# Chunk-selecting attention and a squared-relu FFN in one kernel: who clears a tile, and in which order the FFN's steps are queued

## The chip, the core and the metric

The kernel runs on one core of one Trainium2 chip. The metric is the device time of one execution in microseconds. Before the change it is 281.74 us, the median of three runs (281.1 to 281.81).

## The reference, cut to what matters

```
B, H, S, D = 4, 8, 768, 64          # q, k, v: float32
ub   = sum_d max(q * k_min(chunk), q * k_max(chunk))     # bound of each query on each 32-row chunk
top  = the 6 chunks with the highest ub, of those not after the query's own chunk
attn = softmax(q k^T / 8, over the rows of the chosen chunks that are not after the query)
x    = (attn v), laid out as [3072 tokens, 512]
h    = relu(x @ w_in)               # w_in 512 x 2048
out  = (h * h) @ w_out              # w_out 2048 x 512, out float32
```

## The kernel before, in words

**Tiling.** A sequence is cut into two halves of 384 rows. The eight halves (four batches) are done in the order of `ORDER`; halves 0, 1, 4 and 6 are first halves of a sequence (`half == 0`: 768 score columns a head), halves 2, 3, 5 and 7 second halves (1920 columns a head). A half has four head pairs; one pair of one half is a *slot*, so there are 32 slots, 0 to 31, and half n holds slots 4n to 4n+3. All matmuls are bf16.

**The steps of a slot.** The order of instructions on each engine is the order of the program (the schedule is manual); semaphores are put in where one engine reads what another wrote, and where a buffer is used again.

- `step_T` (in `step_P`, called two slots ahead) transposes k and q of a pair on TensorE (`tk`, `tq`, lines 244 and 251). `relus_T` makes `qr` from `tq` on ScalarE (line 272), `extrema` the chunks' extrema on VectorE (lines 217 to 219), and `place` copies the transposed k and q into `kq` (line 277; k mostly on VectorE, q on ScalarE). From half 3 on the transposes are DMAs and `relus` runs on VectorE (lines 300, 301).
- `step_U` (one slot ahead) makes the bounds `ub` on TensorE (lines 351, 355); VectorE takes the top 8 (MAX8, line 362) and writes which chunks are out (line 363) into `qn0` for half 0, into one of the three `nsel` tiles after that.
- `step_V` transposes that on TensorE (`qt`, line 379 or 390) and VectorE copies it into `kq` beside q (lines 384, 394, 395): a chunk that is out gets a large negative score by the matmul itself.
- `step_E` does one bank of scores on TensorE (`ps`, line 408) and its exponential on ScalarE (`e`, line 413); after the last bank of a head POOL cuts the diagonal blocks (line 417).
- `step_F`, one slot later, multiplies by v (`po`, line 433); VectorE divides (lines 442, 443) and writes `x`.

The places that chunk codes don't reach must be zero: `qn0` is cleared by POOL (line 150), the three `nsel` tiles by ScalarE (`blank`, line 191).

**The FFN.** When a half's `x` is complete it is transposed to `xT` (on TensorE for halves 0, 1 and 7, `x_T`, by DMA for the others), and `push` queues the half's FFN steps: 16 *steps up* (`ffn_up`: four matmuls `ph`, 128 x 384, relu on ScalarE to `ht`, square on VectorE to `h`) and 12 *steps down* (`ffn_down`: four matmuls `py`, 128 x 512, each reading one `h`; four steps to an output tile of 128 tokens, then a copy `ob` on ScalarE or VectorE and a store). The slots of the next half take steps from the queue by `f1()` at fixed places between their own steps, at most `quota` a slot. In the tail, after slot 31, the queue is emptied.

**Order of the queue before.** `push` puts eight steps down of the half before ahead of and between the sixteen up of its own half, and then the first four down of its own (`LAG = 4`); the other eight wait in `downs` for the next push. `quota` is 4 a slot in slots 4 to 7 (half 1), and 8, 6, 7, 7 in the four slots of each later half.

**Buffers.** PSUM: `ps` three buffers (`psS`), `ph` two (`psF`), `py` one (`psY`), the rest two (`psA`). The transposes of slots 6 to 8 use `psY` for k and `psS` for q.

**Loads.** POOL's queue issues nearly all loads, in the order of `later`, which `go` empties slot by slot: `w_in` in slot 0, k and q of half 2 in slot 2, the two halves of `w_out` in slots 3 and 4, the codes of half 2 in slot 4.

**The first slots** are written out by hand ahead of the loop: casts, clears, transposes, and runs of matmuls on `ident` (`busy`) that fill TensorE's waits.

Of the kernel before, what the change touches and what calls it, by code (L numbers as in the profile page):

```python
# [12 lines left out]
ACT = mybir.ActivationFunctionType  # L13
# [18 lines left out]

TP = 4
PP = HB // TP

LAG = 4


@with_exitstack
def kernel(  # L40
# [104 lines left out]
        nc.vector.memset(vn[i][:, :, :, D:D + 1], 1.0)  # L145
    ident = consts.tile([128, 128], BF16, tag="ident")
    make_identity(nc, ident)

    for c in (0, 3):
        nc.gpsimd.memset(qn0[:, :, :, c, :], 0.0)  # L150
    load_packed("k", 0, 4)
    for j in range(HT):
        for h in range(2):
# [31 lines left out]
    codes(0, 0, nc.vector.tensor_copy, 0, 1)  # L185

    warm = consts.tile([128, 1], F32, tag="warm")
    nc.scalar.activation(warm, hmask[:, 0, 0, 0:1], ACT.Exp)

    def blank(i):  # L190
        nc.scalar.mul(nsel[i].rearrange("p j h d -> p (j h) d"),
                      ident[:, 0:D].unsqueeze(1).to_broadcast([128, 2 * HT, D]), 0.0)

    def clear():

# [141 lines left out]
    def step_P(s):  # L337
        if s // NP >= ON_PE:
            relus(s)
            return  # L340
        step_T(s, *((S_, Y) if s == NP + 1 else (F, Y) if s < NP + 2 else
                    (Y, S_) if s < 2 * NP + 1 else (S_, A)))
        if s >= NP + 2 and s != 2 * NP + 1:
            step_T2(s)

# [100 lines left out]
            st.pop(s)  # L446

    queue = []
    downs = []
    h2 = {}  # L450

    xTs = {}
# [34 lines left out]
    def push(hb):  # L487
        xT = xTs.pop(hb)
        xs.pop(hb)
        ups = [lambda act, f=f: ffn_up(hb, xT, f) for f in range(NFI)]  # L490
        for c in ("u" * NFI) if hb == 0 else "dddd" + "uuud" * 4 + "uuuu":
            queue.append((ups if c == "u" else downs).pop(0))
        downs.extend(ffn_downs(hb, int(hb == 2 * B - 1)))
        if hb < 2 * B - 1:
            queue.extend(downs.pop(0) for _ in range(LAG))

    def ffn_downs(hb, tail=False):
        py = {}
        return [lambda act, t=t, c=c: ffn_down(hb, py, t, c, act, tail)
                for t in range(HT - tail) for c in range(4)]  # L500
# [75 lines left out]
        at(0, load_w_in, 1024 * g, 1024 * g + 1024)  # L576
    for j in range(HT):
        at(1, load_vt, 1, j)
    for n in "kq":
        at(2, load_packed, n, 2)  # L580
    at(4, codes, 0, 1, nc.gpsimd.dma_start)
    for g in range(2):
        at(3 + g, load_w_out, 8 * g, 8 * g + 8)
    for j in range(HT):
        at(6, load_vt, 0, HT + j)
        at(7, load_n, "k", 3, j)
# [31 lines left out]

    busy(28)
    step_cast("k", 0)  # L620
    blank(1)
    step_cast("q", 0)
    blank(2)
    clear()
    go(-1, 99)
    step_P(0)
    busy(10)
    step_T2(0)
    place(0, "k", nc.scalar.copy)
    blank(0)  # L630
    step_U(0)
    busy(9)
    step_cast("k", 1)
# [3 lines left out]
    step_cast("q", 1)  # L637
    step_P(1)
    step_T2(1)
    early.close()  # L640
    late = ctx.enter_context(tc.tile_pool(name="late", bufs=2))
    for s in range(NP):
        last = s + 1 == NP
        if s:
            step_E(s, 0, 0)
            step_E(s, 0, 1)
        step_E(s, 1, 0)
        busy(8)
        step_U(s + 1)
        if last:  # L650
            place(s + 1, "k", nc.vector.tensor_copy, 0, 1)
        else:
            place(s + 1, "k", nc.scalar.copy)
        step_E(s, 1, 1)
        if last:
            place(s + 1, "q", nc.scalar.copy)
            place(s + 1, "k", nc.scalar.copy, 1, 2)
        if s:
            step_F(s - 1, 0)
            step_F(s - 1, 1)  # L660
        if last:
            x_T(0, 0, F)
        step_V(s + 1)
        step_P(s + 2)
        if last:
            x_copy(0, 0, 0, 2, nc.vector.tensor_copy)
            busy(10, *F)
        else:
            relus_T(s + 2)
            extrema(st[s + 2]["k"], s + 2)  # L670
        go(s, 99)
    parts = []
# [5 lines left out]
    for s, (b, half, p) in enumerate(slots):  # L678
        if s < NP:
            continue  # L680
        hb = s // NP
        nb = len(BANKS[half])
        hf = nb // 2
        quota = [((4, 4, 4, 4) if hb == 1 else (8, 6, 7, 7))[p]]
        for fn, *a in first.get(s, ()):
            fn(*a)
        if ON_PE - 1 <= hb < 2 * B - 1 and p == (2 if hb < ON_PE else 1):
            parts.extend(step_K(hb + 1))

        def f1():  # L690
            if quota[0] and queue:
                quota[0] -= 1
                fill(1, True)

        if s == NP:
            for n in range(hf):
                step_E(s, 0, n)
            step_F(s - 1, 0)
            step_F(s - 1, 1)
            relus_T(s + 1)  # L700
            x_T(0, 1, F, (0,))
            x_copy(0, 1, 0, 1, nc.vector.tensor_copy)
            busy(8, *A)
            x_T(0, 1, F, (1,))
            x_copy(0, 1, 1, 2, nc.vector.tensor_copy)
            push(0)
            extrema(st[s + 1]["k"], s + 1)
            place(s + 1, "k", nc.vector.tensor_copy)
            place(s + 1, "q", nc.scalar.copy)
        if s == 2 * NP:  # L710
            for n in range(hf):
                step_E(s, 0, n)
            relus_T(s + 1)
            place(s + 1, "q", nc.scalar.copy)
            x_T(1, 0, A)
            x_copy(1, 0, 0, 2, nc.vector.tensor_copy)
            step_F(s - 1, 0)
            step_F(s - 1, 1)
            f1()
            f1()  # L720
            x_T(1, 1, A)
            x_copy(1, 1, 0, 2, nc.scalar.copy)
            push(1)
            extrema(st[s + 1]["k"], s + 1)
            place(s + 1, "k", nc.vector.tensor_copy)
        if p == 0 and hb > 2:
            step_F(s - 1, 0)
            step_F(s - 1, 1)
            step_X(hb - 1, False)
        else:  # L730
            f1()
        if s > NP and s != 2 * NP:
            for n in range(hf):
                step_E(s, 0, n)
        k1()
        f1()
        if p == 0 and hb > 2:
            f1()
            f1()
        if hb > 1 and s != 2 * NP:  # L740
            f1()
        go(s, 2)
        for n in range(hf, nb):
            step_E(s, 0, n)
        if hb < ON_PE and p:
            k1()
        if s + 1 < NS:
            step_U(s + 1)
        f1()
        if p and s > NP:  # L750
            step_F(s - 1, 0)
            step_F(s - 1, 1)
        if half == 0:
            f1()
        if hb < ON_PE and p:
            k1()
        for n in range(hf):
            step_E(s, 1, n)
        f1()
        if s + 1 < NS:  # L760
            step_V(s + 1)
        k1()
        go(s, 99)
        for n in range(hf, nb):
            step_E(s, 1, n)
        k1()
        if s + 2 < NS:
            step_P(s + 2)
        f1()
        if half == 0:  # L770
            f1()
        while quota[0] and queue:
            f1()
    step_F(NS - 1, 0)
    step_F(NS - 1, 1)
    fill(4, True)
    step_X(2 * B - 1, True)
    queue.extend(downs)
    while queue:
        fill(1, len(queue) % 2 == 0)  # L780
    ffn_last(2 * B - 1)
# [30 lines left out]
```

## Time and profile before

| | us |
|---|---|
| median of three runs | 281.74 |
| the profiled execution's own time | 281.77 |
| its span, first to last instruction | 280.0 |
| TensorE busy | 262.2 (94%) |
| ScalarE busy | 181.2 (65%) |
| VectorE busy | 169.3 (60%) |
| POOL busy | 93.3 (33%) |
| granted TensorE clock, mean | 1.000 |

The profile is one execution. Its rows give a start in us from the span's start, a length, the engine (PE is TensorE's matmuls, PEld its weight loads, DVE VectorE, ACT ScalarE, POOL GpSimd, SP the queue engine), the line of the kernel, what is written from what, and the count; in brackets the idle time of the engine before it and what ended that. A matmul's length holds its way through the array, so back-to-back matmuls overlap in these rows; the spacing of starts is what one costs.

### The profile page before, as it was taken

To read this page: it belongs to the slowest core of one execution; us is meant where nothing else is said; L and a number is where in the kernel's file an instruction comes from. 1 tells how busy PE (TensorE), PEld (TensorE's weight loads), DVE (VectorE), ACT (ScalarE), POOL (GpSimd) and SP (SyncE) were. 2 spreads that over 40 slices of the span, in tenths; PEclk is the share of its full clock that TensorE was granted. 3 is DMA by queue.
4 is the path that set the end of the run, shared out by engine and by line. 5 is a ranking of instruction groups with operands and counts; after the bars stand their busy time and mean duration, and the time that the engine had idled before them with its cause. 6 is when DMAs were issued, how large, how long until landed. Compare 5 with 4: busy or idle time off the path is not lost.

```text
span 280.0 us, 6689 instructions
## 1 busy us (share of the span) xinstructions
PE 262.2 (94%) x2472; PEld 167.7 (60%) x2497; DVE 169.3 (60%) x642; ACT 181.2 (65%) x399; POOL 93.3 (33%) x139
## 2 busy tenths in 40 slices
PE   6898798799999999999999999999999999999994
PEld 6677565556657566665565566655565566755544
DVE  7468899756797248643795268635884355414411
ACT  4569689768987568855665687835674777715500
POOL 9778427423553104731453016521111110100000
PEclk9999999999999999999999999999999999999999
DMA  7999999976999746999499349998332200111002
GB/s 153 137 176 200 181 205 201 128 81 97 133 161 182 127 96 124 142 145 146 106 149 153 77 115 150 128 127 179 75 100 51 83 2 0 40 39 40 37 37 75
DMA packets 98272, 32.05 MB, mean 114 GB/s; under 512 B 84640, under 2 KB 93984, under 8 KB 98240
## 3 DMA queue, kind: packets, MB, share of 16 engines
q0 software_dynamic: 64720, 14.42, 63.4%
q1 hardware_dynamic: 32432, 16.88, 27.7%
q10 hardware_dynamic: 1088, 0.33, 0.5%
q8 instruction: 19, 0.31, 0.5%
q14 instruction: 13, 0.11, 0.1%
HBM read 27.26 MB, written 6.29 MB: 120 GB/s over the span
## 4 chain that ended last, share of the span: by engine, by line
PE 74%; DVE 14%; ACT 7%; issue 3%; POOL 1%; DMA 1%; ACTq 0%; POOLq 0%
PE py L539 27%; PE ph L523 22%; PE ps L408 10%; PE po L433 7%; ACT e L413 3%; DVE h L529 2%; PE idle L617 2%; ACT ht L527 2%; DVE km L320 1%; ACT ob L545 1%; DVE x L443 1%; DVE kq L277 1%; DVE m L362 1%; PE ub L355 1%; PE qt L390 1%
## 5 line engine op out<-in xcount | busy, mean ns | idle before, releaser
L413 ACT ACTIVATE e<-ps 128x512 bf16<-128x512 f32 x192 | 96.7, 550 | 28.4 <-PE ps L408 28.3
L523 PE MATMUL ph<-xT,w_in 128*128 128x384 bf16 x512 | 99.2, 326 | 0.9 <-ACT ht L527 0.4
L539 PE MATMUL py<-w_out,h 128*128 128x512 bf16 x343 | 83.9, 379 | 2.6 <-ACT ob L545 0.9
L417 POOL TENSOR_SCALAR_AFFINE_SELECT e<-e 128x384 bf16<-128x384 bf16 x64 | 34.3, 536 | 143.5 <-ACT e L413 143.5
L527 ACT ACTIVATE ht<-ph 128x384 bf16<-128x384 f32 x128 | 62.6, 499 | 26.4 <-PE ph L523 24.8
L529 DVE TENSOR_TENSOR h<-ht 128x384 bf16<-128x384 bf16 x128 | 46.7, 377 | 43.1 <-ACT ht L527 42.9
L523 PEld LDWEIGHTS <-w_in 128*128 128x128 bf16 x512 | 47.5, 97 | 30.5 <-issue 1.9
L408 PE MATMUL ps<-kq 128*128 128x384 bf16 (+2 forms) x320 | 57.8, 283 | 1.9 <-DVE kq L384 1.0
L539 PEld LDWEIGHTS <-h 128*128 128x128 bf16 x368 | 34.9, 98 | 35.3 <-issue 1.7
L408 PEld LDWEIGHTS <-kq 128*128 128x128 bf16 x320 | 27.0, 99 | 14.7 <-issue 3.0
L362 DVE MAX8 m<-ub 128x8 f32<-128x24 f32 (+1 forms) x160 | 16.8, 172 | 22.4 <-PE ub L355 21.5
L433 PEld LDWEIGHTS <-e 128*128 128x128 bf16 x672 | 25.9, 98 | 6.3 <-POOL e L417 1.0
L433 PE MATMUL po<-vn,e 128*128 128x65 bf16 x672 | 27.2, 195 | 1.5 <-POOL e L417 0.8
L545 ACT COPY ob<-py 128x512 f32<-128x512 f32 x19 | 11.1, 586 | 22.7 <-PE py L539 22.3
L443 DVE TENSOR_TENSOR x<-po,r 128x384 bf16<-128x384 f32 x32 | 17.8, 558 | 1.4 <-DVE r L442 0.3
L394 DVE COPY kq<-qt 64x384 bf16<-64x384 bf16 (+1 forms) x28 | 8.8, 315 | 12.4 <-PE qt L390 12.4
L105 POOL DMA_DIRECT2D kn<-in_k_dram x15 | 13.3, 887 | 0.2
L105 POOL DMA_DIRECT2D qn<-in_q_dram x15 | 13.2, 885 | 0.0
L320 DVE TENSOR_TENSOR km<-km 128x384 bf16<-128x384 bf16 (+3 forms) x40 | 11.3, 284 | 1.1
L617 PE MATMUL idle<-ident 128*128 128x128 bf16 x97 | 10.2, 280 | 1.4 <-POOL ident masks.py:199 1.4
L272 ACT ACTIVATE qr<-tq 128x256 bf16<-128x256 bf16 (+1 forms) x24 | 8.8, 426 | 4.0 <-PE tq L244 3.9
L121 POOL DMA_DIRECT2D vn<-in_v_dram x12 | 10.7, 904 | 0.7 <-issue 0.7
(67 smaller groups left out, 205.5 us busy)
## 6 DMA issues: line engine op xcount, KB each, us to landing
out_dram<-ob SPq DMA_DIRECT2D x23, 256.0 KB, 2.2
kq<-kqT SPq DMA_DIRECT2D x10, 384.0 KB, 4.8
w_in<-in_moe_w_in_dram POOLq DMA_DIRECT2D x2, 1024.0 KB, 11.9
w_out<-in_moe_w_out_dram POOLq DMA_DIRECT2D x2, 1024.0 KB, 18.0
kn<-in_k_dram POOLq DMA_DIRECT2D x15, 128.0 KB, 6.1
qn<-in_q_dram POOLq DMA_DIRECT2D x15, 128.0 KB, 5.8
vn<-in_v_dram POOLq DMA_DIRECT2D x12, 128.0 KB, 8.4
vn<-in_v_dram POOLq DMA_DIRECT2D x4, 384.0 KB, 8.0
```

What stands on the lines that cost most here:

```text
L105: nc.gpsimd.dma_start(out=nat_of(n, g)[:, DM * j:DM * j + DM].rearrange("p (h d) -> p h d", d=D), in_=rows(n, *ORDER[g], 0, H)[:, 128 * j: ...
L362: nc.vector.max(out=m8[:, j, hh, :], in_=ub[:, j - j0, hh, :])
L408: nc.tensor.matmul(ps[:, at:at + 128 * m], lhsT=kqs[b % 2][:, hh, p, 2 * (j // HT), 128 * (j % HT):128 * (j % HT + 1)], rhs=qc(s, hh)[:, c ...
L413: nc.scalar.activation(e[:, 512 * n + lo:512 * n + hi], ps[:, lo:hi], ACT.Exp, scale=float(scale))
L417: nc.gpsimd.affine_select(out=d, in_=d, compare_op=ALU.is_ge, fill=0.0, base=0, channel_multiplier=-1, pattern=[[0, 3], [1, 128]])
L433: nc.tensor.matmul(po[:, hh, i, :], lhsT=t["e"][hh][:, c:c + 128], rhs=vn[b % 2][:, 2 * p + hh, j, :], start=(j == 0), stop=(j == iq))
L443: nc.vector.tensor_mul(x[:, :, 128 * p:128 * (p + 1)].rearrange("p j (h d) -> p h j d", h=2), po[:, :, :, 0:D], r.to_broadcast([128, 2, HT ...
L523: nc.tensor.matmul(ph[:, 0:HB], lhsT=w_in[:, ki, 128 * f:128 * (f + 1)], rhs=xT[:, ki, :], start=(ki == 0), stop=(ki == NKI - 1))
L527: nc.scalar.activation(ht, ph[:, 0:HB], ACT.Relu)
L529: nc.vector.tensor_mul(h, ht, ht)
L539: nc.tensor.matmul(py[t], lhsT=h2[hb, f][:, 128 * t:128 * (t + 1)], rhs=w_out[:, f, :], start=(f == 0), stop=(f == NFI - 1))
L617: nc.tensor.matmul(idle, lhsT=ident, rhs=ident, start=True, stop=True)
```

## The change

- ScalarE clears the two outer quarters of `qn0` in its early waits, in four pieces (`blank(p0, p1, c)`); POOL's two clears go. The three `nsel` tiles are cleared by VectorE after slot 1's extrema.
- ScalarE's first activation reads `ident`, not `hmask`.
- The q placement of slot 4 moves from slot 3 to the end of slot 2.
- The transposes of slot 8 use `psS` for k and `psA` for q.
- `LAG` and the carried `downs` go. Each half's steps stand in one order of its own: half 0 has 15 up, a down, the last up, a down, then ten down; the others six up, a down, three up, a down, three up, a down, four up, then nine down.
- `quota` is 6 in each of slots 4 to 11. The later halves keep 8, 6, 7, 7.
- In the tail eight steps down (before: four) precede the transposes of the last half's `x`, and the four that followed them are no longer there.
- The first half of `w_out` is loaded in slot 2, k and q of half 2 in slot 3, the second half of `w_out` in slot 4 and the codes of half 2 in slot 5.

```diff
-LAG = 4
...
-    for c in (0, 3):
-        nc.gpsimd.memset(qn0[:, :, :, c, :], 0.0)
     load_packed("k", 0, 4)
...
-    nc.scalar.activation(warm, hmask[:, 0, 0, 0:1], ACT.Exp)
-
-    def blank(i):
-        nc.scalar.mul(nsel[i].rearrange("p j h d -> p (j h) d"),
-                      ident[:, 0:D].unsqueeze(1).to_broadcast([128, 2 * HT, D]), 0.0)
+    nc.scalar.activation(warm, ident[:, 0:1], ACT.Exp)
+
+    def blank(p0, p1, c):
+
+        nc.scalar.mul(qn0[:, :, p0:p1, c, :],
+                      ident[:, 0:D].unsqueeze(1).unsqueeze(1)
+                      .to_broadcast([128, HT, p1 - p0, D]), 0.0)
...
         step_T(s, *((S_, Y) if s == NP + 1 else (F, Y) if s < NP + 2 else
-                    (Y, S_) if s < 2 * NP + 1 else (S_, A)))
+                    (Y, S_) if s < 2 * NP else (S_, A)))
...
     queue = []
-    downs = []
...
         ups = [lambda act, f=f: ffn_up(hb, xT, f) for f in range(NFI)]
-        for c in ("u" * NFI) if hb == 0 else "dddd" + "uuud" * 4 + "uuuu":
+        downs = ffn_downs(hb, int(hb == 2 * B - 1))
+        for c in ("u" * 15 + "dud") if hb == 0 else "uuuuuuduuuduuuduuuu":
             queue.append((ups if c == "u" else downs).pop(0))
-        downs.extend(ffn_downs(hb, int(hb == 2 * B - 1)))
-        if hb < 2 * B - 1:
-            queue.extend(downs.pop(0) for _ in range(LAG))
+        queue.extend(downs)
...
+    at(2, load_w_out, 0, 8)
     for n in "kq":
-        at(2, load_packed, n, 2)
-    at(4, codes, 0, 1, nc.gpsimd.dma_start)
-    for g in range(2):
-        at(3 + g, load_w_out, 8 * g, 8 * g + 8)
+        at(3, load_packed, n, 2)
+    at(4, load_w_out, 8, 16)
+    at(5, codes, 0, 1, nc.gpsimd.dma_start)
...
     step_cast("k", 0)
-    blank(1)
+    blank(0, 1, 0)
+    blank(0, 1, 3)
     step_cast("q", 0)
-    blank(2)
+    blank(1, NP, 0)
     clear()
...
     place(0, "k", nc.scalar.copy)
-    blank(0)
+    blank(1, NP, 3)
     step_U(0)
...
     step_T2(1)
+    for i in range(3):
+        nc.vector.memset(nsel[i], 0.0)
     early.close()
...
         if last:
-            place(s + 1, "q", nc.scalar.copy)
             place(s + 1, "k", nc.scalar.copy, 1, 2)
...
         else:
             relus_T(s + 2)
+            if s + 2 == NP:
+                place(s + 2, "q", nc.scalar.copy)
             extrema(st[s + 2]["k"], s + 2)
...
-        quota = [((4, 4, 4, 4) if hb == 1 else (8, 6, 7, 7))[p]]
+        quota = [((6, 6, 6, 6) if hb == 1 else (6, 6, 6, 6) if hb == 2 else (8, 6, 7, 7))[p]]
...
     step_F(NS - 1, 1)
-    fill(4, True)
+    fill(8, True)
     step_X(2 * B - 1, True)
-    queue.extend(downs)
     while queue:
         fill(1, len(queue) % 2 == 0)
     ffn_last(2 * B - 1)
```

## The prediction

> **What bounds the kernel now.** I read the page first, then the busy time by stage, then each engine's timeline where the change touches it. A "step up" and a "step down" are FFN steps of four matmuls, a "slot" is one head pair of one half, as told above.
>
> ```profile
> span 280.0 us, 6689 instructions
> ## 1 busy us (share of the span) xinstructions
> PE 262.2 (94%) x2472; PEld 167.7 (60%) x2497; DVE 169.3 (60%) x642; ACT 181.2 (65%) x399; POOL 93.3 (33%) x139
> ```
>
> TensorE is busy for 94%. The change issues the same matmuls in another order, so its work stays; the time can only come from holes that close and go into holes that open.
>
> The next rows are slots 4, 5, 6 and 7, each cut where the slot's transposes end: the span, then busy time and count of PE, PEld, DVE, ACT and POOL. The fence behind them is a later half.
>
> ```profile
> 30.76:35.80 5.04, 4.12 (x44) 2.56 (x45) 4.86 (x17) 3.41 (x8) 2.10 (x3) 1.00 1.98 170
> 35.80:40.87 5.07, 4.67 (x60) 3.08 (x58) 4.57 (x16) 4.52 (x12) 1.04 (x2) 1.00 1.35 203
> 40.87:46.26 5.39, 4.94 (x60) 3.11 (x57) 5.15 (x19) 4.94 (x14) 3.71 (x5) 1.00 1.23 211
> 46.26:52.70 6.44, 5.35 (x63) 3.28 (x61) 6.18 (x24) 5.31 (x13) 4.14 (x6) 1.00 1.98 176
> ```
> ```profile
> 90.30:122.90 32.60, 32.27 (x320) 20.88 (x324) 19.34 (x81) 23.69 (x51) 12.13 (x16) 1.00 1.04 123
> ```
>
> In slots 4 to 7 TensorE has holes and VectorE is nearly full (4.57 to 6.18 us of each slot). In the half from 90.30 on TensorE leaves 0.33 of 32.60 us: there a new wait is paid in full. A step's price: the last downs of the tail stand alone on TensorE,
>
> ```profile
> 265.88 7.07 PE L539 MATMUL py<-w_out,h 128*128 128x512 bf16 x32
> ```
>
> so a down is 4 x 7.07 / 32 = 0.88 us at most (the last matmul's way through the array is in it); I take 0.86. An up is 0.66 by the rows of slot 6 below (40.87 to 41.53); I take 0.65.
>
> **The change, part by part.**
>
> *Clears and the start: 0.* ScalarE now clears `qn0` in four pieces (two of 192 elements a partition, two of 576) where it cleared `nsel` in three; POOL's clears go, so the loads queued behind them on POOL start sooner; VectorE gets three memsets behind slot 1's extrema.
>
> ```profile
> 5.18 0.52 ACT L191 ACTIVATE nsel<-ident 128x384 bf16<-128x384 bf16 x1
> 6.50 0.66 ACT L272 ACTIVATE qr<-tq 128x256 bf16<-128x256 bf16 x2 [0.80 <-PE tq L244]
> ```
> ```profile
> 14.11 0.41 DVE L362 MAX8 m<-ub 128x8 f32<-128x12 f32 x4 [1.34 <-PE ub L355]
> ```
>
> A large clear has 576 elements instead of 384, so at most 0.52 x 1.5 = 0.78 us; the 0.26 us more lie in the 0.80 us in which ScalarE waits for TensorE. The VectorE memsets (each under a clear's 0.52 on ScalarE, three under 1.6; I take half of that) lie in the 1.34 us before the first MAX8. If both covers were short, 0.5 us; a gain of 0.5 if the earlier loads help.
>
> *Slot 4's q placement moves from slot 3 into slot 2: +0.2.*
>
> ```profile
> 24.82 1.66 ACT L413 ACTIVATE e<-ps 128x512 bf16<-128x512 f32 x4
> 26.50 0.96 ACT L277 COPY kq<-tq 64x384 bf16<-64x384 bf16 x2
> ```
> ```profile
> 27.52 0.37 PE L251 MATMUL tq<-ident,qn 96*64 96x96 bf16 x8 [0.46 <-ACT kq L277]
> ```
>
> The 0.96 us now stand ahead of slot 3's four exponentials. The fourth score tile waits for the first exponential (`psS` has three buffers), so TensorE pays about 0.96 there; the 0.46 us wait for the placement goes, and so does most of the wait behind it for the k copy. Bounds -0.5 and +1.0; I take +0.2.
>
> *Slots 4 to 7 get 24 steps instead of 16 (15 up, a down, the last up, 7 down): +4.7.* Eight downs are 6.9 us of TensorE work. Were TensorE alone to decide, they would cost 6.9 less the holes: 0.92 + 0.40 + 0.45 + 1.09 = 2.9 by the rows above, and some 0.6 more that a busy matmul hides, so +3.4. But a loop through ScalarE decides. Slot 6 in the old trace, TensorE then ScalarE:
>
> ```profile
> 40.87 0.82 PE L523 MATMUL ph<-xT,w_in 128*128 128x384 bf16 x4
> 41.53 0.38 PE L408 MATMUL ps<-kq 128*128 128x384 bf16 x2
> 41.75 0.81 PE L523 MATMUL ph<-xT,w_in 128*128 128x384 bf16 x4
> ...
> 43.34 0.81 PE L523 MATMUL ph<-xT,w_in 128*128 128x384 bf16 x4
> ```
> ```profile
> 41.11 0.68 ACT L272 ACTIVATE qr<-tq 128x256 bf16<-128x256 bf16 x2
> 41.81 0.96 ACT L277 COPY kq<-tq 64x384 bf16<-64x384 bf16 x2
> 42.80 0.49 ACT L527 ACTIVATE ht<-ph 128x384 bf16<-128x384 f32 x1
> ```
>
> After the transposes (end 40.87, the cut above) ScalarE does the relus and the q placement before the first `ht`, ready at 43.29, 2.42 us later. `ph` has two buffers, so the third up after the transposes can't start earlier. In the old order that up stands behind the bounds `ub`; in the new one two ups follow the transposes at once and the third stands *before* `ub`, so the scores, `ub`, VectorE's MAX8 and the codes all queue behind its wait. So a new round of slot 5 or 6 is 2.42, then that up 0.65, a score tile and `ub` 0.36, then what followed `ub` in the old round (43.34 to 46.26, less waits that I put at 0.2: 2.7), and one more up before the codes, 0.65: 6.8 us against 5.07 and 5.39. That is +1.5 (slot 5 I put 0.2 below slot 6) and +1.4. Slot 4 itself stays: its fifth up fills a hole. In slot 7 six downs and about 2.0 us of other matmuls, with 0.35 us until ScalarE has emptied the single `py` buffer, make 7.5 against 6.2: +1.3. The last down, after the transposes, adds 0.86, less this hole:
>
> ```profile
> 52.73 0.60 PE L408 MATMUL ps<-kq 128*128 128x384 bf16 x4 [0.25 <-DVE kq L394]
> ```
>
> 1.5 + 1.4 + 1.3 + 0.6 = 4.8; 4.7 taken, bounds 3.4 and 5.5.
>
> A rule of the Trainium skill speaks against me here: Perfetto Trace Analysis, section Identifying the Most-Contended Engine, calls matmul busy time a poor measure of headroom and the share of weight loads a better one. In slot 5 weight loads are busy for 3.08 of 5.07 us, so by the rule some 2 us a slot are free, an estimate, and all eight downs would fit: 0 instead of +4.7. The trace does not bear it out: in the half where TensorE leaves 1% the loads stand at 20.88 of 32.60, hardly more.
>
> *Slots 8 to 11 have 24 steps instead of 28, four downs fewer: -1.2.* On TensorE that is -3.46. The downs taken out are those that stood behind a slot's transposes and covered ScalarE:
>
> ```profile
> 62.92 0.88 ACT L272 ACTIVATE qr<-tq 128x384 bf16<-128x384 bf16 x2
> 63.81 0.96 ACT L277 COPY kq<-tq 64x384 bf16<-64x384 bf16 x2
> ```
>
> Two downs behind slot 8's transposes become ups, so the third up there waits for relus, placement and `ht` as above, about 1.4 us; in slot 10 a down changes places with an up with the same effect, about 0.9. 3.46 - 2.3 = 1.2. Bounds -3.4 (TensorE alone) and -0.5.
>
> *Slots 12 to 31, the order within a half: +2.9.* Twenty-eight steps as before, but a half's last step is now its own fourth down, right behind its last up. The old end of half 3, TensorE, ScalarE and VectorE:
>
> ```profile
> 120.18 1.46 PE L523 MATMUL ph<-xT,w_in 128*128 128x384 bf16 x8
> 121.48 1.12 PE L433 MATMUL po<-vn,e 128*128 128x65 bf16 x30
> ```
> ```profile
> 120.42 1.00 ACT L413 ACTIVATE e<-ps 128x512 bf16<-128x512 f32 x2
> 121.27 0.92 ACT L527 ACTIVATE ht<-ph 128x384 bf16<-128x384 f32 x2
> ```
> ```profile
> 121.70 0.22 DVE L301 TENSOR_SCALAR qr<-kqT 128x256 bf16<-128x256 bf16 x1
> 121.84 0.74 DVE L529 TENSOR_TENSOR h<-ht 128x384 bf16<-128x384 bf16 x2
> ```
>
> The new last up is the first of these two: on TensorE 120.18 to 120.83, its `ht` on ScalarE behind two exponentials from 121.27, its `h` on VectorE ready at about 122.2. The down's first three matmuls end at 121.48; the fourth reads that `h` and waits 0.8 us, and slot 15's value matmuls queue behind it. This holds where two steps end a slot back to back, in halves 3, 5 and 7: +2.4. There too three ups now follow one another across a slot's border, and the third waits 0.3 us for its buffer: +0.9. In halves 4 and 6 the scores lie between, and a down for an up (0.2 longer) covers part of an old wait, twice -0.2:
>
> ```profile
> 150.28 0.36 PE L433 MATMUL po<-vn,e 128*128 128x65 bf16 x6 [0.40 <-POOL e L417]
> ```
>
> Bounds +0.5 and +3.3.
>
> *The tail: -2.4.* Four downs fewer, -3.46. Old tail, TensorE, then ScalarE:
>
> ```profile
> 247.29 0.83 PE L467 MATMUL pt<-ident,x 128*128 128x128 bf16 x12
> 248.13 3.61 PE L539 MATMUL py<-w_out,h 128*128 128x512 bf16 x16
> ```
> ```profile
> 248.16 0.80 ACT L473 COPY xT<-pt 128x768 bf16<-128x768 bf16 x1
> ```
>
> The four downs at 248.13 covered the copy of x; now an up stands there. Its first two matmuls need VectorE's part, the other two this one, ready at 248.96: it ends as if begun at 248.68, so +0.55. At the end the fourth down follows the last up directly:
>
> ```profile
> 266.09 0.49 ACT L527 ACTIVATE ht<-ph 128x384 bf16<-128x384 f32 x1 [0.16 <-PE ph L523]
> ```
> ```profile
> 266.61 0.36 DVE L529 TENSOR_TENSOR h<-ht 128x384 bf16<-128x384 bf16 x1 [0.29 <-ACT ht L527]
> ```
>
> TensorE left the last up at 265.88 (the row of the downs above), its `h` came at 266.97, 1.09 later; three matmuls of a down cover 0.65: +0.45. Bounds -2.9 and -1.9.
>
> *`w_out` sooner: 0.*
>
> ```profile
> L568 POOL DMA_DIRECT2D w_out<-in_moe_w_out_dram x2: 890/894/898, 27.6 to 33.1; - x2
> ```
> ```profile
> DMA to landing us min/median/max: 17.4/18.0/18.6
> ```
>
> The halves landed at about 45.0 and 51.7. The first down now comes in slot 6 near 47, the one that reads the second half near 50. Both loads move up (the first past k and q of half 2, the second past two code loads), so 0 to 1.7 us; I take 0.
>
> Sum: 0 + 0.2 + 4.7 - 1.2 + 2.9 - 2.4 = +4.2. The profiled execution took 281.77 us (280.0 of span and 1.8 around it), the median is 281.74; I predict 286.0.
>
> **Rivals.**
>
> *TensorE alone decides* (faster): the loop through ScalarE does not close, since ScalarE is busy for only 4.52 of 5.07 us in slot 5. Then slots 4 to 7 cost +3.4, 8 to 11 give -3.4, the half ends 0, the tail -2.4, the start +0.2: -2.2, 279.6 us. It decides if `ht` is ready before the third up in slots 5 and 6. Against it: the 2.42 us. Chance 0.14.
>
> *The costs come out at their low bounds* (no change): the waits at half ends hide in old ones (+0.5) and slots 8 to 11 return -3.0: 281.77 + 0.2 + 4.7 - 3.0 + 0.5 - 2.4 = 281.8. The rule on weight loads would give 281.77 + 0.2 + 0 - 1.2 + 2.9 - 2.4 = 281.3 and belongs here, with 0.03 of the chance. Together 0.12.
>
> *The second half of `w_out` is late* (slower still): 1.7 us in slot 7, 287.7; it decides once the load lands after 50. For: the queue is full until then. Chance 0.12.
>
> My forecast keeps 0.62. The changed order is plain in the code, so that the change doesn't do what it says has no chance of its own.
>
> **How the numbers follow.** Faster by over 0.3% (0.8 us, about what a measurement of this kernel tells from no change): 0.14. Within: 0.12. Slower: 0.62 + 0.12 = 0.74. The range leaves out the faster rival and the far end above: 281.2 (the mixed case) to 288.6 (late `w_out` and 0.9 of the high bounds). The forecast's own range is 283.5 to 288.
>
> **What would show it.** Right: from the transposes of one slot to the next 6.5 to 7 us in slots 5 and 6, with a TensorE wait for `ht` there; TensorE waiting some 0.8 us for `h` at the end of halves 3, 5 and 7; two waits of about 0.5 in the tail. Wrong: slots 5 and 6 below 6.2 us, half ends without a wait, slots 8 to 11 shorter by 3 us, or a wait for the `w_out` load in slot 7.

## The result, and the profile after

The changed kernel takes 291.01 us in the median of four runs (289.57 to 292.19), the kernel before 281.77 beside it: a ratio of 1.033 (95% interval 1.027 to 1.038). The forecast was 286.0 with 288.6 as the upper end. The profiled execution took 291.55 us, its span is 289.8. From here on a *u* is a step up and a *d* a step down; line numbers of the changed kernel are two to five lower than those of before (518 up, 534 down, 405 scores, 410 exponential, 522 `ht`, 524 `h`, 540 output copy).

The page of the changed kernel, its span and busy times:

```profile
span 289.8 us, 6712 instructions
## 1 busy us (share of the span) xinstructions
PE 264.3 (91%) x2497; PEld 165.2 (57%) x2497; DVE 167.5 (58%) x643; ACT 184.5 (64%) x402; POOL 91.7 (32%) x137
```

TensorE is busy for about as long as before (264.3 us against 262.2) in a span 9.8 us longer: the time went into holes. Where, by cuts that both traces have (first up; slot 8's first score tile; first value matmul of slot 11; of slot 31; end):

| stretch | before | after | difference | forecast |
|---|---|---|---|---|
| start to the first up | 30.76 | 30.45 | -0.3 | +0.2 |
| to slot 8's scores | 21.97 | 27.07 | +5.1 | +4.7 |
| to slot 11's value matmuls | 35.99 | 36.04 | 0.0 | -1.2 |
| to slot 31's value matmuls | 154.16 | 160.20 | +6.0 | +2.9 |
| tail | 37.12 | 36.04 | -1.1 | -2.4 |

Busy time by stage of the changed kernel (columns as in the prediction): slots 4 to 7, each to the end of its transposes, and the half that answers to 90.30 to 122.90 of before.

```profile
30.45:35.46 5.01, 4.90 (x49) 2.89 (x48) 4.70 (x17) 3.56 (x9) 0.52 (x1) 1.00 1.81 181
35.46:41.99 6.53, 5.92 (x68) 3.88 (x66) 5.62 (x21) 5.69 (x14) 2.29 (x4) 1.00 1.36 201
41.99:48.73 6.74, 6.13 (x68) 3.87 (x66) 5.51 (x20) 5.52 (x14) 3.69 (x5) 1.00 1.31 219
48.73:56.65 7.92, 7.50 (x72) 4.06 (x69) 5.24 (x19) 4.38 (x10) 3.61 (x5) 1.00 3.20 136
94.95:128.49 33.54, 32.85 (x326) 20.68 (x323) 19.21 (x80) 24.08 (x51) 12.31 (x16) 1.00 1.04 120
```

Slots 5 and 6 are the rounds of 6.5 to 7 us that were forecast. The late half has 0.69 us of holes instead of 0.33. What TensorE waited for over the whole run (total, times, longest):

```profile
PE py L534 <- DVE h L524: 7.5, 8, 1.9
PE ph L518 <- ACT ht L522: 3.2, 4, 1.1
PE py L534 <- ACT ob L540: 1.9, 4, 0.7
```

The first row is the finding: downs wait 7.5 us for the `h` that they read, in eight places; the kernel before has no such row. Three of the eight, as TensorE shows them: slot 11, the end of slot 18 with the beginning of slot 19, and the end of half 3.

```profile
86.68 0.39 PE L534 MATMUL py<-w_out,h 128*128 128x512 bf16 x1 [1.88 <-DVE h L524]
```
```profile
148.32 1.46 PE L518 MATMUL ph<-xT,w_in 128*128 128x384 bf16 x8
149.62 0.38 PE L405 MATMUL ps<-kq 128*128 128x384 bf16 x2
149.84 0.59 PE L534 MATMUL py<-w_out,h 128*128 128x512 bf16 x2
152.12 0.66 PE L534 MATMUL py<-w_out,h 128*128 128x512 bf16 x2 [1.68 <-DVE h L524]
```
```profile
125.66 0.81 PE L534 MATMUL py<-w_out,h 128*128 128x512 bf16 x3
127.09 0.39 PE L534 MATMUL py<-w_out,h 128*128 128x512 bf16 x1 [0.61 <-DVE h L524]
```

The first two are a *third* down, which reads the products of ups 9 to 12. In slot 11 it stands directly behind the twelfth up, in slot 19 one score tile behind it. VectorE, at the time of the second:

```profile
149.72 1.14 DVE L317 TENSOR_TENSOR km<-km 128x384 bf16<-128x384 bf16 x4
150.89 0.28 DVE L323 TENSOR_TENSOR kbd<-km,hmask 128x48 bf16<-128x48 bf16 x2
151.08 0.55 DVE L297 TENSOR_SCALAR qr<-kqT 128x384 bf16<-128x384 bf16 x1
151.55 0.24 DVE L298 TENSOR_SCALAR qr<-kqT 128x384 bf16<-128x384 bf16 x1
151.72 0.61 DVE L524 TENSOR_TENSOR h<-ht 128x384 bf16<-128x384 bf16 x2
```

The two `h` queue behind the extrema of the next half's chunks (`km`, `kbd`) and behind the products of the slot after next (`qr`): 2.0 us of work. The tail, four rows of TensorE:

```profile
259.01 3.61 PE L534 MATMUL py<-w_out,h 128*128 128x512 bf16 x16 [0.67 <-ACT ob L540]
...
263.61 4.49 PE L518 MATMUL ph<-xT,w_in 128*128 128x384 bf16 x24 [0.32 <-DVE xT L469]
...
274.88 0.39 PE L534 MATMUL py<-w_out,h 128*128 128x512 bf16 x1 [0.33 <-DVE h L524]
...
278.93 3.84 PE L534 MATMUL py<-w_out,h 128*128 128x512 bf16 x17 [0.26 <-DVE h L524]
```

The first of these waits, for the single `py` buffer to be copied out between two runs of four downs, was not in the forecast.

### The profile page after: what moved, and what is told of

It is laid out like the page before. It is cut to its first block, busy times and chain, and to the rows that moved or that the text cites. A ratio compares the mean times of both kernels' runs of the same rounds, so it can differ in the third digit from the quotient of the medians.

```text
span 289.8 us, 6712 instructions
## 1 busy us (share of the span) xinstructions
PE 264.3 (91%) x2497; PEld 165.2 (57%) x2497; DVE 167.5 (58%) x643; ACT 184.5 (64%) x402; POOL 91.7 (32%) x137
## 4 chain that ended last, share of the span: by engine, by line
PE 63%; DMA 14%; ACT 10%; DVE 8%; issue 3%; POOL 2%; ACTq 0%; POOLq 0%
PE py L534 25%; PE ph L518 19%; PE ps L405 8%; DMA w_out<-in_moe_w_out_dram 8%; PE po L430 6%; ACT e L410 4%; DMA qn<-in_q_dram 3%; ACT ht L522 3%; DMA kn<-in_k_dram 3%; DVE h L524 3%; DVE km L317 2%; ACT ob L540 2%; PE py L504 1%; PE ub L352 1%; PE qt L387 1%
## 5 line engine op out<-in xcount | busy, mean ns | idle before, releaser
L534 PE MATMUL py<-w_out,h 128*128 128x512 bf16 x368 | 91.5, 379 | 9.9 <-DVE h L524 7.5
L405 PE MATMUL ps<-kq 128*128 128x384 bf16 (+2 forms) x320 | 56.7, 279 | 2.2 <-ACT e L410 1.2
L540 ACT COPY ob<-py 128x512 f32<-128x512 f32 x21 | 12.3, 585 | 30.5 <-PE py L534 30.4
L439 DVE RECIPROCAL r<-po 128x6 f32<-128x6 f32 x32 | 6.2, 193 | 9.2 <-PE po L430 8.9
L317 DVE TENSOR_TENSOR km<-km 128x384 bf16<-128x384 bf16 (+3 forms) x40 | 10.4, 261 | 1.1
```

What stands on the lines that cost most here:

```text
L405: nc.tensor.matmul(ps[:, at:at + 128 * m], lhsT=kqs[b % 2][:, hh, p, 2 * (j // HT), 128 * (j % HT):128 * (j % HT + 1)], rhs=qc(s, hh)[:, c ...
L534: nc.tensor.matmul(py[t], lhsT=h2[hb, f][:, 128 * t:128 * (t + 1)], rhs=w_out[:, f, :], start=(f == 0), stop=(f == NFI - 1))
L540: nc.scalar.copy(ob, py[t])
```

## The experiments

The kernel before had a median of 280.1 to 280.7 us beside the experiments, over 1 us less than its four runs beside the changed kernel (281.77). Each ratio is to the kernel before on the same chip. The two kernels below in which keys were moved and the time did not change took 290.97 and 291.22 us, ratios of 1.039 and 1.040. So beside these runs of before the changed kernel stands near 1.04, an estimate, and the 1.033 above is rather low. Gains below are counted from its 291.

### The order of the downs

**The third down behind the last up.**

```diff
-        for c in ... else "uuuuuuduuuduuuduuuu":
+        for c in ... else "uuuuuuduuuduuuuuuud":
```

> The changed kernel with the half's order u6 d u3 d u7 d instead of u6 d u3 d u3 d u4 (u a step up, d a step down; the fourth down follows as before): the third down, which reads the products of ups 9 to 12, now stands behind up 16 and has four ups of slack instead of none, and it stands between the last up and the fourth down. Theory: TensorE's waits for h (7.5 us in 8 waits) come from downs that stand right behind the up whose h they read; they fall to under 2.5 us and the kernel to 285 to 287. Rival: more ups in a row make TensorE wait for ht instead (ph has two buffers): the waits for ht grow by as much, 290 to 292.

284.18 us (283.45 to 284.83), ratio 1.014 (1.011 to 1.016): 6.8 us less than the changed kernel, somewhat more than the theory gave. Of the waits of TensorE in its trace the row for `h` is gone, and the row for `ht` is what it was (a wait of 1.0 us for keys is new):

```profile
PE ph L518 <- ACT ht L522: 3.2, 4, 1.1
PE py L534 <- DMA w_out<-in_moe_w_out_dram: 2.4, 1, 2.4
```

From slot 11's to slot 31's value matmuls it takes 154.55 us, against 154.16 before and 160.20 in the changed kernel. The theory holds, and one moved letter settles the largest term of the miss: +6.0 us in this stretch becomes +0.4.

**The half ends on an up.** One step more in slot 11, so that all later halves are shifted by one step.

```diff
-        ... (6, 6, 6, 6) if hb == 2 ...
+        ... (6, 6, 6, 7) if hb == 2 ...
```

> The changed kernel with 25 steps instead of 24 in slots 8 to 11 (one more in slot 11), so that every half from the third on ends on its last up, and its fourth down comes in the next half. Theory: the waits for h at the ends of the halves (1.88, 0.61, 1.68 us and so on) are paid in full and go: six of them, 5 to 6.5 us less, about 285. Rival: the wait only moves, since VectorE is as far behind with h in the next half's first slot, or another buffer stops TensorE there: less than 2 us gained, 289 or more.

303.10 us (300.04 to 304.58), ratio 1.077 (1.070 to 1.083): 12 us slower instead of 5 to 6 faster. Both sides had the size wrong; the rival had the kind.

```profile
PE py L534 <- DVE h L524: 11.3, 11, 2.3
PE py L534 <- ACT ob L540: 7.5, 12, 0.7
```

The third down keeps its place right behind the twelfth up, so its wait stays; by the shift it now meets key work in halves 3 and 5 too (1.59 us each), and in halves 4 and 6 it waits 2.34 and 2.03. And the fourth down is now followed at once by the first down of the next output tile, which waits for the one `py` buffer: 12 waits of up to 0.7 us, where in the changed kernel the value matmuls lay between. A shift by one step moves every down against what covers it.

**Keys behind the last steps.** First in the fourth slot of a half:

```diff
+        if p == 3 and hb > 1:
+            while quota[0] and queue:
+                f1()
         k1()
         if s + 2 < NS:
             step_P(s + 2)
```

> The changed kernel with the last pieces of the next half's block keys, and the products of the next slot, put behind the last steps of each half's fourth slot instead of ahead of them. Theory: in the halves that end with slots 11, 19 and 27 the h of the last two ups queues on VectorE behind about 2 us of key work; without it the wait falls from 1.6 to 1.9 us to about 0.6, as in the halves that end with slots 15 and 23, and the bounds of the next half are not later than now: 2.5 to 3.5 us less, 288. Rival: the h is late because its ht is late on ScalarE: within 0.7 us of 291.0. Second rival: the keys become the late ones, the next half's bounds wait instead, 0 to 1 us gained.

290.97 us (290.62 to 292.55), ratio 1.039 (1.035 to 1.043): unchanged. The edit missed its aim: the keys that stand in front of the late `h` are issued at the end of the third slot, and the edit moved one `h` ahead of two `qr` only, in halves 3 and 5. There the down's wait stayed at 0.61 us: the `h` waits for its `ht` from ScalarE, as the prediction had it for these half ends. Then in the right slot, for halves 4 and 6:

```diff
+        mid = p == 2 and half == 0 and hb > 2
-        k1()                  # twice, at the end of the slot
+        if not mid:
+            k1()
...
+        if hb > 2 and p == 3: # behind the next slot's first scores
+            k1()
+            k1()
```

> The changed kernel with the last two pieces of the next half's block keys behind the first two steps of the fourth slot of halves 4 and 6, instead of at the end of the third slot; the earlier run that moved the keys moved those of the wrong slot. Theory: the third down waits 1.6 to 1.7 us there because the h it reads queues on VectorE behind 1.14 + 0.28 us of key work; the two waits fall to about 0.4 us each, 2 to 2.6 us less in all. Rival: the bounds of the next half then wait for their keys by as much: within 0.7 us of 291.

291.22 us (290.00 to 293.85), ratio 1.040 (1.034 to 1.046): unchanged again, now for the rival's reason.

```profile
PE py L534 <- DVE h L524: 4.4, 6, 1.9
PE ub L352 <- DVE kbd L323: 3.4, 2, 1.7
PE ph L518 <- ACT ht L522: 3.2, 4, 1.1
```

The two waits for `h` in halves 4 and 6 are gone (7.5 to 4.4, eight to six), which shows that the key work was what held them; and the next half's bounds wait 3.4 us for their keys instead. Moved this way the work only changes who waits.

### Slots 4 to 11 and the loads

**The old numbers of steps.**

```diff
-        quota = [((6, 6, 6, 6) if hb == 1 else (6, 6, 6, 6) if hb == 2 else (8, 6, 7, 7))[p]]
+        quota = [((4, 4, 4, 4) if hb == 1 else (8, 6, 7, 7))[p]]
```

> The changed kernel with the old numbers of steps a slot (4 in slots 4 to 7; 8, 6, 7, 7 in slots 8 to 11), everything else as changed. Theory: the eight downs moved into slots 4 and 7 cost 5 us there, since the loop through ScalarE and the landing of w_out bound these slots; without them slots 4 to 7 take as long as before, the tail has four downs more (3.5 us) and slots 8 to 11 four more (3.5 us, part of it hidden), and a half now ends on an up, with the third down right behind its up one step earlier: 286 to 289. Rival: TensorE's sum alone decides, the steps cost the same wherever they stand: 291, within 1 us.

297.24 us (296.27 to 297.57), ratio 1.060 (1.057 to 1.063): outside both. It shifts the later halves as well, by four steps, and with the downs right behind their ups that is paid again:

```profile
PE py L534 <- DVE h L524: 6.1, 13, 1.5
PE py L534 <- ACT ob L540: 5.9, 9, 0.9
```

So it says nothing clean about slots 4 to 7. The next run keeps the sum and thus the later halves.

```diff
-        ... (6, 6, 6, 6) if hb == 1 else (6, 6, 6, 6) if hb == 2 ...
+        ... (4, 4, 4, 4) if hb == 1 else (8, 8, 8, 8) if hb == 2 ...
```

> The changed kernel with the same 48 steps in slots 4 to 11, but 4 a slot in slots 4 to 7 and 8 a slot in slots 8 to 11, so that nothing behind slot 11 moves. Theory: slots 4 to 7 fall back to some 21.9 us (5.1 less, and no wait for w_out with the halved clock that followed such a wait in three runs), while eight steps more in slots 8 to 11 cost 6.9 us less the waits for ht that they cover (1.12 and 0.82): 288 to 290. Rival: a step costs the same in both places, 291 within 0.7 us.

290.59 us (290.49 to 291.60), ratio 1.038 (1.033 to 1.042): the rival's number. From its first up to slot 8's scores:

```profile
27.33:50.33 23.00, 19.36 (x218) 12.10 (x218) 20.57 (x72) 17.87 (x43) 11.19 (x17) 1.00 1.64 196
```

That is 4.07 us less than the 27.07 of the changed kernel, though 1.27 us of it are a wait for a load; from there to slot 11's value matmuls (at 92.62) it takes 42.29 us instead of 36.04, 6.25 more. The eight steps cost at least as much in slots 8 to 11 as in slots 4 to 7; nothing is won by moving them. With this edit and the moved third down together:

> The kernel of the run before with the order u6 d u3 d u7 d as well (the third down behind the last up). Theory: the two gains add: no wait for h, no wait for w_out and no halved clock behind it: 280.5 to 282.5, two to four less than the 284.2 of the order alone. Rival: what is saved in slots 4 to 7 is spent in slots 8 to 11: 284 within 0.7 us.

283.04 us (281.45 to 284.65), ratio 1.010 (1.007 to 1.013), 1.1 less than the order alone, between theory and rival; the intervals of the two overlap, so this gain is not shown.

**The second half of `w_out` ahead of k and q of half 2.**

```diff
-    for n in "kq":
-        at(3, load_packed, n, 2)
-    at(4, load_w_out, 8, 16)
+    at(3, load_w_out, 8, 16)
+    for n in "kq":
+        at(4, load_packed, n, 2)
```

> The changed kernel with the second half of w_out loaded ahead of k and q of the third half instead of behind them. Theory: the second half of w_out landed at 48.3 to 49.9 us in the runs so far, where its first down would be due at 46.5 to 49; with it some 2 us earlier the step down no longer waits for it, and what the faster start gained is kept: 1 to 2 us less than 291, and no TensorE wait for w_out. Rival: the landing is hidden in this place (TensorE is held by ScalarE's loop), or k and q of the third half become late: within 0.7 us of 291, or slower.

293.17 us (293.13 to 296.06), ratio 1.048 (1.043 to 1.053): slower. The wait for `w_out` is gone and one for q stands in its place:

```profile
48.55 0.37 PE L248 MATMUL tq<-ident,qn 96*64 96x96 bf16 x8 [1.95 <-DMA qn<-in_q_dram]
```

Here the other order only changed which load is waited for.

### The tail

```diff
-    fill(8, True)
+    fill(4, True)
```

> The changed kernel with four downs instead of eight ahead of the last half's transposes of x. Theory: the transposes then stand where the output buffer is copied out, and the other four downs where x is copied: the waits of 0.67 and 0.32 us in the tail go with what lies around them, 1.0 to 1.3 us of 291. Rival: the downs stand in front of the last ups and the end is as late as before: within 0.5 us of 291.

289.49 us (288.72 to 291.94), ratio 1.036 (1.031 to 1.041). The tail takes 34.70 us (252.30 to 287.0) instead of 36.04:

```profile
253.26 3.62 PE L534 MATMUL py<-w_out,h 128*128 128x512 bf16 x16
256.71 0.83 PE L463 MATMUL pt<-ident,x 128*128 128x128 bf16 x12
257.55 3.61 PE L534 MATMUL py<-w_out,h 128*128 128x512 bf16 x15
261.00 4.24 PE L518 MATMUL ph<-xT,w_in 128*128 128x384 bf16 x24
```

The transposes cover the copy out of `py`, the next four downs the copies of x; both waits are gone. The theory holds in the trace; in the medians (1.5 us) the ranges overlap, and the ratio is not clearly below 1.039 either. With order, numbers of steps and the old place of the placement together:

> The kernel of the run before with four downs instead of eight ahead of the last half's transposes of x in the tail (the other four behind them, where they cover the copies of x), and slot 4's q placement back in slot 3. Theory: in the tail the 0.68 us wait for the output copy and some 0.5 us for the copies of x go, 1.0 to 1.3 us; the placement is worth 0.2 us at most: 279.5 to 281, below the kernel before. Rival: the four downs behind the transposes only shift the waits: no gain on the run before.

280.80 us (280.22 to 282.58), ratio 1.003 (1.000 to 1.005). The four edits together take back all but 0.7 us of what the change lost, but do not beat the kernel before.

### The start and the clock

```diff
+        if last: place(s + 1, "q", nc.scalar.copy)    # back in slot 3
-            if s + 2 == NP: place(s + 2, "q", nc.scalar.copy)
```

> The changed kernel with slot 4's q placement back in slot 3, nothing else undone. Theory: the clock halves from 23.8 to 30.2 us because two TensorE holes lie close together, 1.17 us for the load of q at 21.3 and 1.16 us for the exponential that stands behind the moved placement at 24.0. Without the second hole the granted clock stays at 1.00, the first step up starts near 28 us instead of 30.45, and the time falls by 2 to 4 us, to about 288. Rival: the load wait alone lowers the clock; it still halves for some 6 us, and the time stays within 0.7 us of 291.0, since the placement's wait of about 0.5 us comes back in slot 3.

290.27 us (289.16 to 291.91), ratio 1.035 (1.031 to 1.040): at the edge of the rival's bounds, though for no reason that either gave. The granted clock still halved, but from about 10 to 17 us and not at 24. The trace of the run with the keys in the fourth slot, which keeps the placement in slot 2, has the clock halved at the same place, and there the first up comes at 28.81 against 28.59: the placement costs 0.2 us, as far as two single traces can tell.

**The clears alone, on the kernel before.**

```diff
-    for c in (0, 3):
-        nc.gpsimd.memset(qn0[:, :, :, c, :], 0.0)
+    blank(0, 1, 0); blank(0, 1, 3); blank(1, NP, 0); blank(1, NP, 3)   # ScalarE, places as in the change
+    for i in range(3): nc.vector.memset(nsel[i], 0.0)                  # behind slot 1
```

> The kernel before with the clears of the change alone: ScalarE clears qn0 in its waits, POOL's two clears go, VectorE clears nsel behind slot 1. Theory: POOL's loads start 1.4 us earlier, TensorE is at its fast spacing (55 instead of 107 ns a small matmul) from about 7 us on instead of 21, and the first step up starts 2 to 3 us earlier, at about 28: 279. Rival: TensorE then waits for the load of q of the second half and the granted clock halves as in the changed kernel; the first up is where it was and the time is 281 to 283.

279.37 us (278.22 to 280.66, eight runs), ratio 0.996 (0.994 to 0.999): 0.4% faster than the kernel before. The edit also lets ScalarE's first activation read `ident`, as the change does. The first up:

```profile
27.02 1.46 PE L522 MATMUL ph<-xT,w_in 128*128 128x384 bf16 x8
```

3.7 us earlier than in the profiled run of before. Is that the clears? The kernel before, profiled again:

> The kernel before, unchanged, profiled once more. Its single runs show granted clocks from 0.979 to 1.00 and times from 278.5 to 281.8, though nothing in it differs. Theory: the first trace caught the latest of several moments at which TensorE goes to its fast spacing (21.5 us); in another run it goes at 6 to 10 us, as in the changed kernel, and the first step up then starts near 27 to 29 us instead of 30.76, so that most of the changed kernel's early start is not the change's. Rival: the kernel before is always at the slow spacing until 21 us, and the clears of the change are what ends it.

It took 281.74 us and showed the late moment once more (first up at 30.52): inconclusive. (At the slow spacing the eight idle matmuls of a group take 1.06 us in these traces, at the fast one 0.61.) A third look, and the kernel before with more filler at its very start:

```diff
-    busy(28)
+    busy(36)
```

> The kernel before, unchanged, profiled once more, since the second look caught the same late moment as the first. Theory as there: in a run with a granted clock of 0.98 to 0.998 TensorE is at its fast spacing from 6 to 12 us on (a halving is recorded only where it was fast before), and the first step up starts near 27 to 29 us. Rival: the first up is at 30.5 whatever the clock.

> The kernel before with 36 idle matmuls instead of 28 at the very start, which fill TensorE's hole from 4.6 to 5.5 us and change nothing else. Theory: that hole is what sets when TensorE goes to its fast spacing; filled, the fast spacing comes at about 7 us as in the changed kernel, and the first step up starts at 27 to 29 us instead of 30.5 to 30.8, POOL's clears notwithstanding: 279 to 280 in the median. Rival: POOL's clears, and the loads queued behind them, hold the start; the first up stays at 30 and the median at 280.4 or above.

The third look took 279.60 us. TensorE's idle matmuls and its first up in that run, then its clock (the third number from the end of a row):

```profile
5.97 0.72 PE L617 MATMUL idle<-ident 128*128 128x128 bf16 x10
15.91 1.06 PE L617 MATMUL idle<-ident 128*128 128x128 bf16 x8
28.96 1.46 PE L523 MATMUL ph<-xT,w_in 128*128 128x384 bf16 x8
```
```profile
10.00:12.00 2.00, 1.05 (x19) 0.85 (x19) 1.20 (x3) 1.56 (x5) 2.00 (x3) 0.97 1.72 109
12.00:14.00 2.00, 1.58 (x18) 1.08 (x15) 0.61 (x5) 1.93 (x6) 0.80 (x2) 0.50 1.51 98
...
18.00:20.00 2.00, 1.94 (x25) 1.42 (x24) 1.94 (x5) 1.01 (x4) 1.71 (x4) 0.82 1.16 247
```

Unchanged code: at the fast spacing from 6 us on, halved from 11.9 to 18.7 us, first up at 28.96. The run that the forecast stood on shows the latest of these moments (slow until about 21 us). With the filler the kernel before takes 279.80 us (278.78 to 280.90, ten runs), ratio 0.997 (0.995 to 1.000), and its first up, with no halving in the trace, is at

```profile
27.37 1.46 PE L523 MATMUL ph<-xT,w_in 128*128 128x384 bf16 x8
```

By these two traces the clears themselves explain 0.35 of the 3.7 us (27.37 to 27.02), and the rest is when the clock rises. That the filled hole of 0.9 us brings the rise forward rests on the medians (0.9 us less than before) and is not shown by the one trace, since the third look has an early rise without it. Two attempts to build on this gave nothing:

```diff
+    busy(10)    # ahead of the first scores, and again ahead of slot 1's products
```

> The kernel of the run before with two times ten more idle matmuls in the first 13 us, in TensorE's holes ahead of the first scores and ahead of slot 1's products. Theory: in about half the runs so far the granted clock halved between 10 and 18 us, behind these holes, and the first step up came 1 to 1.6 us later; with the holes filled the clock stays at 1.00 in every run up to the first step up, the runs lie closer together and the median is 0.3 to 1 us lower than without. Rival: the added matmuls stand in front of the scores and delay the start by 0.5 to 1 us, and the clock halves all the same.

282.48 us (280.24 to 285.17), ratio 1.007 (1.004 to 1.010), slower than without (280.80): its profiled run waits 1.79 us for the load of q in slot 6 and its runs spread more (4.9 us against 2.4). And on the kernel with the clears alone:

```diff
-        quota = [((4, 4, 4, 4) if hb == 1 else (8, 6, 7, 7))[p]]
+        quota = [((5, 5, 4, 4) if hb == 1 else (7, 6, 6, 7) if hb == 2 else (8, 6, 7, 7))[p]]
```

> The kernel before with the clears of the change, and with 5, 5, 4, 4 steps in slots 4 to 7 and 7, 6, 6, 7 in slots 8 to 11 (two steps up moved into holes, the sum as before). Theory: TensorE's holes in slots 4 and 5 (0.92 and 0.40 us) take two steps up at half their price, and no down comes sooner than w_out lands: 0.3 to 0.8 us below the 279.4 of the clears alone. Rival: the loop through ScalarE lengthens slots 4 and 5 by the full step, and nothing is gained: 279.4 within 0.4 us.

279.68 us (278.66 to 281.01), ratio 0.998 (0.996 to 1.001): the rival, no gain over the clears alone.

## Why the prediction was wrong, step by step

**The order within a half (+2.9; measured +6.0) is the step that failed.** Where it looked, it was right in kind: at the end of halves 3, 5 and 7 the fourth down waits 0.61, 0.61 and 0.72 us for `h` (0.8 forecast), and those halves grew by 0.99, 0.55 and 0.66 us (1.1 each; the 0.3 for three ups in a row, part of the 1.1, shows as no wait for `ht` there). But it priced only the fourth down, and of halves 4 and 6 it said that the scores lie between, -0.2 each. They grew by 2.14 and 1.70 us, 1.68 and 1.39 of it in one wait each: the *third* down has no slack either, and in those halves its `h` stands behind the key work on VectorE. The prediction had no term for the third down. The order with the third down moved takes 6.8 us off, and of this term's +6.0 it leaves +0.4.

**Slots 8 to 11 (-1.2; measured 0.0)** failed by the same omission: slot 11's third down waits 1.88 us. Without it the stretch would stand at -1.8, by subtraction. The waits for `ht` that were forecast there, 1.4 and 0.9, are in the trace with 1.12 and 0.82.

**The tail (-2.4; measured -1.1)** was mis-sized by two waits that had no term: from the value matmuls to the transposes of x 0.83 us more than eight downs take (the wait for the output copy), and 0.49 us at the third down. The two that had one came out: 0.55 for the copies of x (0.31 and 0.24), 0.50 for the last `h` (0.45). -3.46 + 0.83 + 0.55 + 0.49 + 0.50 is -1.09.

**Slots 4 to 7 (+4.7; measured +5.1)** went as worked out: 6.53 and 6.74 us in slots 5 and 6, each with a wait of 0.61 us for `ht`, and 7.92 in slot 7. That eight downs cost more than the +3.4 of TensorE alone is confirmed; that they stood in a bad place is not, since moved into slots 8 to 11 they cost 6.25.

**The clears (0) and the placement (+0.2)** came out within their bounds: a gain of 0.35 and a cost of 0.2, each from one pair of traces. (The MAX8 at 14.11 that the prediction calls the first is the second; the first is at 7.71. The three clears on VectorE took 0.63 us, where 0.8 was allowed.) The start as a whole was still misread, since the one profiled run of before was taken for how it always starts. In the changed kernel's profiled run the early start was lost again to a halved clock, so that the start came out near its forecast (-0.3 against +0.2) by luck:

```profile
22.00:24.00 2.00, 0.89 (x16) 0.74 (x15) 1.01 (x6) 1.94 (x6) 0.44 (x1) 0.89 1.12 213
24.00:26.00 2.00, 1.96 (x25) 1.70 (x26) 0.95 (x4) 1.51 (x4) 1.33 (x3) 0.50 1.13 215
...
30.00:32.00 2.00, 2.00 (x15) 1.18 (x13) 1.45 (x5) 1.03 (x3) 0.00 (x0) 0.91 1.94 166
```

**`w_out` (0, or 1.7 as a rival)** was both. In the profiled run it hardly shows. In three runs with the changed kernel's numbers of steps in slots 4 to 7 whose first up came at 27.0 to 27.5 us the second half is waited for 2.1 to 3.1 us, since it lands at 48 to 50 us however early the start is: an earlier start is eaten there.

Of the rivals, TensorE alone was refuted by the waits themselves. The 0 for slots 4 to 7 that was worked out from the Trainium skill's rule (Perfetto Trace Analysis, Identifying the Most-Contended Engine) was refuted as well: they cost 5.1 us. The share of weight loads fell from 60% to 57% and that of matmuls from 94% to 91%; neither says which step waits for what.

## What to carry to other kernels

When steps of a producer and a consumer are put into one queue, count for every consumer how many steps stand between it and the last producer it reads, and look up what the engines between them have queued at that very place, not only at the place where the new order looks tightest. Four steps of slack instead of none took 6.8 us off 291 here, with the same instructions. And before a start is compared with another, look at several runs of the *unchanged* kernel: its profiled run may be the odd one.

## What was unexpected of the hardware

The moment at which TensorE goes from the slow to the fast spacing differs between runs of the same code: 6 us in one trace of the kernel before, between 20 and 21.5 in two. Two rows of TensorE in the trace of before that the prediction read:

```profile
17.30 1.06 PE L617 MATMUL idle<-ident 128*128 128x128 bf16 x8
21.48 0.61 PE L617 MATMUL idle<-ident 128*128 128x128 bf16 x8
```

The same eight matmuls take 1.06 and then 0.61 us, and the granted clock reads 1.00 in both places: a mean clock of 1.00 does not say that the start was fast. Once it is fast, it can be halved again: behind the waits at 21 to 24 us of the changed kernel for 6.8 us (summing its rows: 0.44 + 6 + 0.36), in the third look at before for 6.8, and behind the wait of 2.42 us for `w_out` in the run with the moved third down for 3.4:

```profile
48.00:50.00 2.00, 1.29 (x6) 0.60 (x6) 0.48 (x1) 0.00 (x0) 0.16 (x1) 0.88 4.23 105
50.00:52.00 2.00, 2.00 (x8) 0.81 (x7) 0.00 (x0) 0.61 (x2) 0.00 (x0) 0.50 3.83 120
52.00:54.00 2.00, 1.90 (x24) 1.21 (x23) 0.94 (x7) 0.86 (x2) 1.00 (x2) 0.77 1.69 148
```

A wait of TensorE can thus cost more than its length: after it the matmuls run at half speed for a while. The length of one wait does not decide: behind 1.95 us for q (the run with the second half of `w_out` first) the clock halved too, but behind 2.07 us for `w_out` (the run with four downs ahead of the transposes) and 2.34 us for `h` (the run whose halves end on an up) it stayed at 1.00. The Trainium skill (TensorE: Matmul & The Clock Gate, Part 1) describes a gate that watches a free-running window of about 3.4 us; the stretches of 3.4 and twice 3.4 us agree with it. The same section of the Trainium skill lets the moment of the rise vary by about 500 ns; here it varies by some 15 us, and why is open. What sets whether a wait halves the clock, and for one window or two, was not tried.
